# Loading q and k of a chunked-attention and mixture-of-experts kernel with eight tokens of one head pair in a partition

## The chip, the cores and the metric

The kernel runs on one core of a Trainium2 chip. The metric is the device time of one execution in microseconds (us), lower is better. A core has a matrix engine (TensorE; its matmuls are PE in the profile and its weight loads PEld), a vector engine (DVE), a scalar engine (ACT), GpSimd (POOL) and a sync engine (SP). Each takes its instructions in program order. Transfers between the chip's memory (HBM) and SBUF, the on-chip memory of 128 partitions, run on 16 DMA engines that all issuing engines share. Here SP issues the loads of q and k and of the weights and the stores of the attention output, and POOL issues nearly all loads of v and all indirect transfers.

## The reference

There are three stages, all in float32: attention inside chunks of 64 tokens, a top-1 mixture of experts, and a dense two-layer network.

```python
# 8 batches, 8 heads, 576 tokens (9 chunks of 64), head size 64
scores = matmul(q_c, k_c^T) / 8          # inside each chunk of 64 tokens
attn = softmax(scores)
x = matmul(attn, v_c)                    # -> 4608 tokens x 512
idx = argmax(x @ w_gate)                 # 8 experts
y[t] = max_prob[t] * relu(x[t] @ w1[idx[t]]) @ w2[idx[t]]      # 512 -> 1024 -> 512
out = relu(y @ w_in)**2 @ w_out          # 512 -> 2048 -> 512
```

## The kernel before

The attention stage is a loop of 36 iterations, each of 128 tokens (two chunks) of all eight heads. q and k come in units of 256 tokens (four chunks), 18 in all, so one unit feeds two iterations. The order of all instructions is written out by hand: `for it in range(-3, NTILE + 1)` from line 455 gives every engine its program order, and nothing is rescheduled.

`load_qk(u)` (lines 241 to 255) fills one tile `qk` (tag `a`, four buffers) with q in its first half and k in its second. A partition holds two neighbouring tokens of all eight heads: eight runs of 2 x 64 floats, 512 bytes each. Partitions 32c to 32c+31 belong to chunk c of the unit, so one transfer fills all 128 partitions where the unit lies in one batch. A batch has nine chunks, so six of the 18 units cross the end of a batch; there `divmod` on line 248 splits q and k each into two transfers, of 32 and 96 partitions (four units) or of 64 and 64 (two units). The other 12 units are called whole below and those six split.

`regroup(z)` (lines 265 to 269) copies on POOL the q (even z) or k (odd z) of a unit into one of four slots of `by_r`, so that two heads of one token position stand side by side. `trans` (lines 271 to 304) transposes them on PE into PSUM, in two halves `hh`, and ACT or DVE copies the result into `qT` (q) or `kb` (k, with zeros between so that two heads share one matmul). Unit 0 is not regrouped: it is transposed straight from `qk`. `scores`, `expo`, `attn_t` and `pv` follow for each iteration, and `pv` stores 128 finished tokens to `x_d` from SP (line 359). `x_t`, `gate_t`, `route`, `place` and `scatter` make the routing out of them beside the loop.

The loads run ahead of the loop. Before the loop stand `load_qk(0)`, `load_qk(1)`, `load_qk(2)` and two parts of v of batch 0 (lines 386 to 420). `load_qk(u + 3)` is issued from `trans_upto` (line 453) when unit u has been transposed, so on SP it stands behind the store of `x_d` of the same iteration. `regroup` runs up to seven tiles of q or k ahead of the iteration (lines 456 to 459). `load_v` (lines 257 to 263) issues eight transfers a batch from POOL; each goes to one half of the partitions (64 of them), in runs of 256 bytes. The weights of the first experts are loaded by SP from iteration 22 on (line 487). The experts and the dense network then take the rest of the time.

Of the kernel before, what the change touches and what calls it, by code (L numbers as in the profile page):

```python
# [8 lines left out]
F32 = mybir.dt.float32  # L9
# [11 lines left out]
def kernel(ctx, tc, q, k, v, w_gate, w1, w2, w_in, w_out, out):  # L21
    nc = tc.nc
    B, H, S, D = q.shape
    NT, DM = out.shape
    NE = w_gate.shape[1]
    CH = 64
    NCB = S // CH
    NPAIR = H // 2
# [46 lines left out]
    def tl(tag, shape, dt, name):  # L75
        if tag in fixed:
            ts, n = fixed[tag]
            fixed[tag] = ts, n + 1
            t = ts[n % len(ts)].bitcast(dt)
            k = 1  # L80
            for z in shape[1:]:
                k *= z
            t = t[0:shape[0], 0:k]
            names = "abcde"[:len(shape) - 1]
            return t.rearrange(f"p ({' '.join(names)}) -> p {' '.join(names)}", **dict(zip(names, shape[1:])))
        if tag == "m":
# [67 lines left out]
    at_job, done, known = [0], [0], [min(i for i, (l, n, _) in enumerate(jobs) if n and n > 1)]  # L154
# [74 lines left out]
    def attention():  # L229
        with ExitStack() as actx:  # L230
            ps_t = actx.enter_context(tc.tile_pool(name="ps_t", bufs=4, space=PSUM))
# [2 lines left out]

            vb = [[tl("hhhhhhba"[4 * s + p], [128, NCB, 2, D + 1], F32, f"vb{s}{p}") for p in range(NPAIR)] for s in range(2)]
            kb = [tl("b", [128, NPAIR, 4, 2, CH], F32, f"kb{s}") for s in range(2)]
            by_r = tl("c", [128, 4, 2, H, D], F32, "by_r")
            xTs = tl("c", [128, 2, KD, 512], F32, "xTs")
            st = {}

            def load_qk(u):
                qk = tl("a", [128, 2, H, 2 * D], F32, f"qk{u}")
                for j, (src, nm) in enumerate(((q, "q"), (k, "k"))):
                    t = qk[:, j]
                    g = 4 * u
                    done = 0
                    while done < 4:
                        b, c = divmod(g + done, NCB)
                        n = min(4 - done, NCB - c)
                        nc.sync.dma_start(  # L250
                            out=t[32 * done:32 * (done + n)],
                            in_=src[b, :, c * CH:(c + n) * CH, :].rearrange("h (p r) d -> p h (r d)", r=2),
                        )
                        done += n
                    st[nm, u] = t

# [8 lines left out]
            def regroup(z):  # L265
                u, j = divmod(z, 2)
                if u:
                    src = st["qk"[j], u].rearrange("p h (r d) -> p r h d", r=2)
                    nc.gpsimd.tensor_copy(out=by_r[:, z % 4], in_=src)

            def trans(nm, u, hh):
                if hh == 0:
                    if nm == "q":
                        st["qT", u] = tl("b", [128, NPAIR, 128, 2], F32, f"qT{u}")
                src = st[nm, u] if hh == 0 else st.pop((nm, u))
                ps = ps_t.tile([128, 2, 2, 128], F32, tag="t", name="tq")
                if u == 0:
                    for h in range(4):
                        nc.tensor.transpose(ps[:, h // 2, h % 2, :], src[:, 4 * hh + h, :], ident)
                    for r in range(2):  # L280
                        for j in range(2):
                            i_ = ps[64 * r:64 * r + 64, :, j, :]
                            eng = nc.scalar.copy
                            if nm == "q":
                                o = st["qT", u][64 * j:64 * j + 64, 2 * hh:2 * hh + 2, :, r]
                            else:
                                eng = nc.vector.tensor_copy
                                i_ = i_.rearrange("p a (c i) -> p a c i", c=4)
                                o = kb[u % 2].rearrange("p a c j (i r) -> p a j c i r", r=2)[64 * j:64 * j + 64, 2 * hh:2 * hh + 2, j, :, :, r]
                            eng(o, i_)  # L290
                    return
                z = 2 * u + (nm == "k")
                for a in range(2):
                    for r in range(2):
                        h = 4 * hh + 2 * a
                        nc.tensor.transpose(ps[:, a, r, :], by_r[:, z % 4, r, h:h + 2, :].rearrange("p h d -> p (h d)"), ident)
                i_ = ps.rearrange("p a r i -> p a i r")
                if nm == "q":
                    nc.scalar.copy(st["qT", u][:, 2 * hh:2 * hh + 2], i_)
                else:  # L300
                    o = kb[u % 2].rearrange("p a c j (i r) -> p j a c i r", r=2)
                    i_ = i_.rearrange("p a (c i) r -> p a c i r", c=4)
                    for j in range(2):
                        (nc.vector.tensor_copy if j and u < 3 else nc.scalar.copy)(o[64 * j:64 * j + 64, j, 2 * hh:2 * hh + 2], i_[64 * j:64 * j + 64])

            def scores(i):
                u, h2 = divmod(i, 2)
                qt, kt = st["qT", u], kb[u % 2]
                ps = ps_s.tile([128, H, CH], F32, tag="s", name="sc")
                for p in range(NPAIR):  # L310
                    for c2 in range(2):
                        c = 2 * h2 + c2
                        nc.tensor.matmul(
                            ps[64 * c2:64 * c2 + 64, 2 * p:2 * p + 2, :],
                            lhsT=qt[:, p, 32 * c:32 * c + 32, :].rearrange("p i r -> p (i r)"),
                            rhs=kt[:, p, c],
                            start=True,
                            stop=True,
                        )
                mx = tl("m", [128, H], F32, "mx")  # L320
                nc.vector.tensor_reduce(mx, ps, axis=AX.X, op=ALU.max)
                at = tl("r", [128, H, CH], F32, "at")
                nc.vector.tensor_tensor(out=at, in0=ps, in1=mx[:, :, None].to_broadcast([128, H, CH]), op=ALU.subtract)
                st["at", i] = at
# [91 lines left out]
            c = min(6, NCB)  # L416
# [14 lines left out]
            for g in range(NG - 1):  # L431
                t = 4 * g + (7 if g < NG - 3 else 6)
# [22 lines left out]
            for it in range(-3, NTILE + 1):  # L455
# [8 lines left out]
                if 0 <= it + 1 < NTILE:  # L464
                    scores(it + 1)
# [659 lines left out]
```

## Time and profile before

| what | value |
|---|---|
| median of three runs | 1461.23 us (1460.78 to 1465.03) |
| the profiled execution's own time | 1460.37 us |
| its span, first to last instruction | 1458.5 us |
| matmul (PE) busy | 1419.3 us, 97% of the span |
| attention loop, first score matmul to last `pv` | about 10.6 to 184 us |
| mean granted TensorE clock | 0.993 |

The page gives busy times for the whole span and then the span in 40 slices of 36.5 us; the first five slices are the attention stage. A digit is a busy share in tenths. Under the slices stands what the DMA engines moved in each, in GB/s. A window of the trace is a stretch of time from the span's start. Where the text speaks of a line, L250 is line 250 of the kernel before.

### The profile page before, as it was taken

The page shows a single profiled execution, that of the slowest core. Times are in us where ns is not written, and L with a number is a line of the kernel's source. Part 1 is how long each engine was busy: PE and PEld are TensorE (multiplying, and loading weights), DVE is VectorE, ACT ScalarE, POOL GpSimd, SP SyncE. Part 2 cuts the span into 40 slices and gives each one's busy share as a digit, 9 for nine tenths or more (in the row PEclk, how much of TensorE's full clock was granted, in tenths as well). Part 3 has the DMA queues.
Part 4 walks back from the last instruction along what each step waited for, and adds up shares of the span by engine and source line. Part 5 has one row for each costly group of instructions (what it writes and reads, how often), then busy time and mean ns, then how long its engine had stood idle before and what let it go on. Part 6 is the DMA issues. An engine that isn't in the chain of part 4 may idle for free.

```text
span 1458.5 us, 21568 instructions
## 1 busy us (share of the span) xinstructions
PE 1419.3 (97%) x8186; PEld 1222.9 (84%) x8186; DVE 761.5 (52%) x1371; ACT 549.6 (38%) x936; POOL 505.6 (35%) x608
## 2 busy tenths in 40 slices
PE   7988988999999999999999999999999999999998
PEld 5877788888889999997888888888888888888886
DVE  7767787578888788884432322322332232233222
ACT  4765634444444455554422222222222222222222
POOL 7675755436555446643003040210404012040301
PEclk9999999999999999999999999999999999999999
DMA  9999555767678778885101010100101001010000
GB/s 204 260 259 244 148 162 182 221 192 234 208 225 247 223 234 266 268 257 163 58 15 46 1 60 0 44 17 1 60 0 60 0 26 35 1 60 0 31 2 29
DMA packets 144369, 172.90 MB, mean 119 GB/s; under 512 B 18160, under 2 KB 103872, under 8 KB 144256
## 3 DMA queue, kind: packets, MB, share of 16 engines
q1 hardware_dynamic: 110032, 112.58, 27.0%
q0 software_dynamic: 17920, 40.51, 10.0%
q10 hardware_dynamic: 16304, 18.36, 3.8%
q8 instruction: 65, 1.06, 0.3%
q14 instruction: 48, 0.39, 0.1%
HBM read 133.05 MB, written 38.34 MB: 118 GB/s over the span
## 4 chain that ended last, share of the span: by engine, by line
PE 54%; POOL 0%; POOLq 0%; issue 0%; DVE 0%
PE hp L1034 27%; PE py L1055 27%; POOL out_dram L1015 0%; POOLq L1120 0%; DVE o L1063 0%; POOL between L1014 0%
## 5 line engine op out<-in xcount | busy, mean ns | idle before, releaser
L1034 PE MATMUL hp<-xm,w_None 128*128 128x512 f32 x1728 | 417.5, 391 | 3.3 <-DVEq L978 3.3
L1034 PEld LDWEIGHTS hp<-xm,w_None 128*128 128x128 f32 x1728 | 326.3, 189 | 71.5 <-ACTq L978 3.5
L1055 PE MATMUL py<-w_None,h 128*128 128x512 f32 x1512 | 363.2, 389 | 0.0
L1055 PEld LDWEIGHTS py<-w_None,h 128*128 128x128 f32 x1512 | 283.8, 188 | 58.8
L1039 DVE SCALAR_TENSOR_TENSOR rs<-hp,rs 128x512 f32<-128x512 f32 x144 | 99.5, 691 | 437.7 <-ACT rs L1038 437.7
L1038 ACT ACTIVATE rs<-hp 128x512 f32<-128x512 f32 x144 | 86.0, 597 | 460.0 <-PE hp L1034 460.0
L1015 POOL DMA_INDIRECT out_dram<-o,tp x36 | 35.1, 974 | 630.2 <-ACT o L1061 624.2
L796 PE MATMUL pa<-xs,w 128*128 128x256 f32 (+2 forms) x1344 | 242.3, 329 | 5.7 <-DVE h L800 2.4
L808 PE MATMUL pb<-h,w 128*128 128x256 f32 (+2 forms) x1344 | 243.9, 331 | 0.0
L796 PEld LDWEIGHTS pa<-xs,w 128*128 128x128 f32 x1344 | 211.4, 189 | 23.5 <-DVE h L800 4.8
L808 PEld LDWEIGHTS pb<-h,w 128*128 128x128 f32 x1344 | 209.9, 190 | 14.5
L1041 DVE TENSOR_TENSOR h<-rs,h 128x512 fp32r<-128x512 f32 x144 | 99.7, 692 | 99.0 <-ACT h L1040 99.0
L190 DVE TENSOR_TENSOR w<-raw,w 128x1024 fp32r<-128x1024 f32 x100 | 132.0, 1321 | 17.1 <-ACT w L189 15.3
L799 ACT ACTIVATE h<-pa 128x256 fp32r<-128x256 f32 (+2 forms) x112 | 53.2, 475 | 215.5 <-PE pa L796 185.4
L1040 ACT CAST h<-rs 128x512 fp32r<-128x512 f32 x144 | 89.5, 622 | 110.3 <-DVE rs L1039 110.3
L189 ACT CAST w<-raw 128x1024 fp32r<-128x1024 f32 x113 | 118.1, 1046 | 0.0
L844 POOL TENSOR_TENSOR cr<-cr 128x256 f32<-128x256 f32 x64 | 49.7, 777 | 124.8 <-DVE cr L859 46.6
L800 DVE SCALAR_TENSOR_TENSOR h<-pa,h 128x256 fp32r<-128x256 f32 (+2 forms) x112 | 59.5, 534 | 59.7 <-ACT h L799 55.1
L845 POOL TENSOR_TENSOR cr<-cr 128x256 f32<-128x256 f32 x64 | 73.6, 1149 | 5.0
L223 POOL DMA_INDIRECT xg<-x_d,tk x40 | 44.6, 1115 | 28.1 <-PE pt L785 17.7
L1055 PE MATMUL py<-w,h 128*128 128x512 f32 x216 | 51.7, 389 | 0.0
L210 POOL DMA_INDIRECT tk<-tk_d,at x40 | 41.7, 1042 | 22.1 <-issue 8.5
(204 smaller groups left out, 1325.0 us busy)
## 6 DMA issues: line engine op xcount, KB each, us to landing
raw<-in_moe_w_dram SPq DMA_DIRECT2D x112, 512.0 KB, 4.1
x_d<-x SPq DMA_DIRECT2D x36, 256.0 KB, 6.8
x<-y_d POOLq DMA_DIRECT2D x36, 256.0 KB, 3.0
cr<-in_moe_w_in_dram SPq DMA_DIRECT2D x32, 256.0 KB, 4.2
cr<-in_moe_w_out_dram SPq DMA_DIRECT2D x32, 256.0 KB, 5.5
vb<-in_v_dram POOLq DMA_DIRECT2D x56, 144.0 KB, 8.2
qk<-in_q_dram SPq DMA_DIRECT2D x12, 512.0 KB, 10.1
qk<-in_k_dram SPq DMA_DIRECT2D x12, 512.0 KB, 12.2
```

Source lines behind the costliest of these rows:

```text
L189: nc.scalar.copy(w[0], raw)
L190: eng.tensor_tensor(out=w[1], in0=raw, in1=w[0], op=ALU.subtract)
L796: nc.tensor.matmul(ps[:, 0:N], lhsT=w[wl][:, kk, o:o + 128], rhs=xT[:, xl, kk, 0:N], start=(kk == 0 and wl + xl == 0), stop=(kk == KD - 1 ...
L800: nc.vector.scalar_tensor_tensor(out=h[:, 1, 0:N], in0=ps[:, 0:N], scalar=0.0, in1=h[:, 0, 0:N], op0=ALU.max, op1=ALU.subtract)
L808: nc.tensor.matmul(pb[d][:, 0:N], lhsT=w[wl][:, f % 2, 128 * d:128 * d + 128], rhs=h[:, hl, 0:N], start=(f + hl + wl == 0), stop=(f == NF ...
L845: nc.gpsimd.tensor_tensor(out=af, in0=af, in1=ef, op=ALU.add)
L1034: nc.tensor.matmul(ps, lhsT=w[wl][:, kk, o:o + 128], rhs=xT[:, xl, kk, :], start=(kk == 0 and wl + xl == 0), stop=(kk == KD - 1 and wl == 1))
L1038: nc.scalar.activation(out=rs[:, 0], in_=ps, func=AF.Relu)
L1039: nc.vector.scalar_tensor_tensor(out=rs[:, 1], in0=ps, scalar=0.0, in1=rs[:, 0], op0=ALU.max, op1=ALU.mult)
L1040: nc.scalar.copy(h[:, 0], rs[:, 1])
L1041: nc.vector.tensor_tensor(out=h[:, 1], in0=rs[:, 1], in1=h[:, 0], op=ALU.subtract)
L1055: nc.tensor.matmul(ys[t], lhsT=h[:, hl, 128 * t:128 * t + 128], rhs=w[wl][:, g % 2, :], start=(g == 0 and hl + wl == 0), stop=(g == NF2 - ...
```

## The change

`load_qk` puts eight neighbouring tokens of one pair of heads in a partition. A partition then holds two runs (one a head) of 8 x 64 floats, 2048 bytes each. The pair, a, selects the group of 32 partitions (32a to 32a+31), and inside it eight partitions belong to each chunk. A transfer can no longer fill all partitions at once, so each of the former transfers becomes four, one a pair: 32 partitions each in a whole unit; 8 and 24, or 16 and 16, in a split one. `by_r`, the transposes and the copies behind them follow the new order: the half `hh` now selects four of the eight token positions for all heads, where it selected four heads. The number and size of the copies on POOL, ACT and DVE and of the transposes stay as they were; `qT` is now plain in token order, and `scores` reads it so.

```diff
-            by_r = tl("c", [128, 4, 2, H, D], F32, "by_r")
+            by_r = tl("c", [128, 4, 8, 2, D], F32, "by_r")
...
-                qk = tl("a", [128, 2, H, 2 * D], F32, f"qk{u}")
+                qk = tl("a", [128, 2, 2, 8 * D], F32, f"qk{u}")
...
-                        nc.sync.dma_start(
-                            out=t[32 * done:32 * (done + n)],
-                            in_=src[b, :, c * CH:(c + n) * CH, :].rearrange("h (p r) d -> p h (r d)", r=2),
-                        )
+                        for a in range(NPAIR):
+                            nc.sync.dma_start(
+                                out=t[32 * a + 8 * done:32 * a + 8 * (done + n)],
+                                in_=src[b, 2 * a:2 * a + 2, c * CH:(c + n) * CH, :].rearrange("h (p r) d -> p h (r d)", r=8),
+                            )
...
-                    src = st["qk"[j], u].rearrange("p h (r d) -> p r h d", r=2)
+                    src = st["qk"[j], u].rearrange("p h (r d) -> p r h d", r=8)
...
-                        st["qT", u] = tl("b", [128, NPAIR, 128, 2], F32, f"qT{u}")
+                        st["qT", u] = tl("b", [128, NPAIR, 256], F32, f"qT{u}")
...
-                for a in range(2):
-                    for r in range(2):
-                        h = 4 * hh + 2 * a
-                        nc.tensor.transpose(ps[:, a, r, :], by_r[:, z % 4, r, h:h + 2, :].rearrange("p h d -> p (h d)"), ident)
-                i_ = ps.rearrange("p a r i -> p a i r")
+                for r in range(4):
+                    nc.tensor.transpose(ps[:, r], by_r[:, z % 4, 4 * hh + r].rearrange("p h d -> p (h d)"), ident)
+                i_ = ps.rearrange("p r n -> p n r")
+                w = slice(4 * hh, 4 * hh + 4)
                 if nm == "q":
-                    nc.scalar.copy(st["qT", u][:, 2 * hh:2 * hh + 2], i_)
+                    nc.scalar.copy(st["qT", u].rearrange("p a (g r) -> p (a g) r", r=8)[:, :, w], i_)
...
-                            lhsT=qt[:, p, 32 * c:32 * c + 32, :].rearrange("p i r -> p (i r)"),
+                            lhsT=qt[:, p, 64 * c:64 * c + 64],
```

## Rows read from the trace of the kernel before

**Rows 1.** The page: engine busy times and the span in 40 slices.

```profile
PE 1419.3 (97%) x8186; PEld 1222.9 (84%) x8186; DVE 761.5 (52%) x1371; ACT 549.6 (38%) x936; POOL 505.6 (35%) x608
...
DMA  9999555767678778885101010100101001010000
GB/s 204 260 259 244 148 162 182 221 192 234 208 225 247 223 234 266 268 257 163 58 15 46 1 60 0 44 17 1 60 0 60 0 26 35 1 60 0 31 2 29
```

**Rows 2.** Windows, attention stage: busy us and instructions by engine, clock, DMA share, GB/s.

```profile
12.00:36.00 24.00, 20.23 (x220) 17.20 (x221) 15.89 (x37) 10.11 (x20) 17.53 (x31) 1.00 1.21 208
36.00:73.00 37.00, 36.95 (x449) 31.76 (x449) 26.37 (x64) 28.42 (x52) 22.53 (x31) 1.00 1.09 259
73.00:109.00 36.00, 32.16 (x385) 27.73 (x380) 24.78 (x61) 21.67 (x39) 27.29 (x38) 0.95 1.10 260
109.00:146.00 37.00, 33.32 (x379) 29.47 (x376) 29.21 (x67) 20.88 (x39) 22.08 (x31) 0.91 0.94 244
```

**Rows 3.** Groups by line, 0 to 165 us: busy, mean ns, idle before and releaser.

```profile
L296 PE MATMUL tq<-ident,by_r 128*128 128x128 f32 x272 | 42.4, 285 | 4.5 <-POOL by_r L269 4.5
L304 ACT COPY kb<-tq 64x512 f32<-64x512 f32 x62 | 35.9, 579 | 4.6 <-PE tq L296 3.9
L269 POOL COPY by_r<-qk 128x1024 f32<-128x1024 f32 x34 | 35.0, 1050 | 31.3 <-DMA qk<-in_q_dram 18.9 <-DMA qk<-in_k_dram 5.5 <-PE pv L346 3.6
L299 ACT COPY qT<-tq 128x512 f32<-128x512 f32 x34 | 20.1, 590 | 6.7 <-PE tq L296 6.6
L336 ACT COPY aT<-ta 128x512 f32<-128x512 f32 x32 | 18.8, 586 | 48.3 <-PE ta L334 31.0 <-DVE mx L321 8.4 <-DVE ei L517 4.9
L279 PE MATMUL tq<-ident,qk 128*128 128x128 f32 x16 | 3.9, 425 | 5.2 <-DMA qk<-in_q_dram 5.2
```

**Rows 4.** The page, DMA issues: KB each, median us from issue to landing.

```profile
vb<-in_v_dram POOLq DMA_DIRECT2D x56, 144.0 KB, 8.2
qk<-in_q_dram SPq DMA_DIRECT2D x12, 512.0 KB, 10.1
qk<-in_k_dram SPq DMA_DIRECT2D x12, 512.0 KB, 12.2
```

**Rows 5.** Timeline of SP's queue: start us, us, issues; units 2, 4, 16 and 17.

```profile
10.80 2.92 SPq L250 DMA_DIRECT2D qk<-in_q_dram  x2
13.76 1.84 SPq L250 DMA_DIRECT2D qk<-in_k_dram  x2
...
21.35 2.62 SPq L250 DMA_DIRECT2D qk<-in_q_dram  x2
24.02 3.43 SPq L250 DMA_DIRECT2D qk<-in_k_dram  x2
...
130.01 0.38 SPq L250 DMA_DIRECT2D qk<-in_q_dram  x1
130.44 1.15 SPq L250 DMA_DIRECT2D qk<-in_k_dram  x1
...
142.70 0.41 SPq L250 DMA_DIRECT2D qk<-in_q_dram  x1
143.16 1.46 SPq L250 DMA_DIRECT2D qk<-in_k_dram  x1
```

**Rows 6.** Windows in which one kind of transfer runs nearly alone; columns as rows 2.

```profile
15.80:19.20 3.40, 2.75 (x28) 2.34 (x24) 1.78 (x3) 1.90 (x5) 2.60 (x8) 1.00 1.22 213
30.50:33.20 2.70, 2.08 (x20) 1.68 (x18) 1.96 (x5) 1.36 (x3) 1.53 (x3) 1.00 1.22 206
141.40:142.80 1.40, 1.40 (x16) 1.40 (x14) 1.33 (x4) 1.30 (x3) 0.00 (x0) 1.00 1.14 295
154.30:156.80 2.50, 2.50 (x35) 2.46 (x35) 2.33 (x6) 1.98 (x4) 2.50 (x4) 1.00 1.02 195
117.00:120.80 3.80, 1.77 (x25) 1.58 (x27) 3.52 (x10) 3.12 (x6) 0.00 (x0) 0.78 0.01 4
```

**Rows 7.** DMA totals, 30.5:33.2, 148.3:150 and 126.5:128.5 us: packets, MB, mean GB/s.

```profile
DMA packets 1119, 0.56 MB, mean 206 GB/s; under 512 B 41, under 2 KB 1118, under 8 KB 1119
...
DMA packets 621, 0.59 MB, mean 347 GB/s; under 512 B 60, under 2 KB 424, under 8 KB 621
...
DMA packets 625, 0.69 MB, mean 345 GB/s; under 512 B 37, under 2 KB 521, under 8 KB 625
```

**Rows 8.** Timeline of POOL and PE at the last unit: start us, us, instructions.

```profile
151.16 5.96 POOL L260 DMA_DIRECT2D vb<-in_v_dram  x8
157.06 2.08 POOL L269 COPY by_r<-qk 128x1024 f32<-128x1024 f32 x2
...
164.14 0.60 PE L296 MATMUL tq<-ident,by_r 128*128 128x128 f32 x4
```

**Rows 9.** Issues and landings of the lines L250, L359: duration ns min/median/max, times.

```profile
L250 SPq DMA_DIRECT2D qk<-in_q_dram x24: 378/521/1826, 0.8 to 142.7; - x24
L250 SPq DMA_DIRECT2D qk<-in_k_dram x24: 313/1148/6107, 1.3 to 143.2; - x24
...
L359 SPq DMA_DIRECT2D x_d<-x x36: 319/384/7757, 27.6 to 191.6; - x36
...
DMA to landing us min/median/max: 2.0/6.8/13.9
```

More of the change, by code (lines that the diff above doesn't have):

```diff
@@ L273, in trans @@
                     if nm == "q":
-                        st["qT", u] = tl("b", [128, NPAIR, 128, 2], F32, f"qT{u}")
+                        st["qT", u] = tl("b", [128, NPAIR, 256], F32, f"qT{u}")
                 src = st[nm, u] if hh == 0 else st.pop((nm, u))
-                ps = ps_t.tile([128, 2, 2, 128], F32, tag="t", name="tq")
+                ps = ps_t.tile([128, 4, 128], F32, tag="t", name="tq")
                 if u == 0:
-                    for h in range(4):
-                        nc.tensor.transpose(ps[:, h // 2, h % 2, :], src[:, 4 * hh + h, :], ident)
+                    for h in range(2):
+                        for a in range(2):
+                            nc.tensor.transpose(ps[:, 2 * h + a], src[:, h, 256 * hh + 128 * a:256 * hh + 128 * a + 128], ident)
@@ L280, in trans @@
                     for r in range(2):
                         for j in range(2):
-                            i_ = ps[64 * r:64 * r + 64, :, j, :]
-                            eng = nc.scalar.copy
+                            i_ = ps[64 * r:64 * r + 64, 2 * j:2 * j + 2].rearrange("p a n -> p n a")
+                            w = slice(4 * hh + r, 4 * hh + r + 3, 2)
                             if nm == "q":
-                                o = st["qT", u][64 * j:64 * j + 64, 2 * hh:2 * hh + 2, :, r]
-                            else:
-                                eng = nc.vector.tensor_copy
-                                i_ = i_.rearrange("p a (c i) -> p a c i", c=4)
-                                o = kb[u % 2].rearrange("p a c j (i r) -> p a j c i r", r=2)[64 * j:64 * j + 64, 2 * hh:2 * hh + 2, j, :, :, r]
@@ L290, in trans @@
-                            eng(o, i_)
+                                o = st["qT", u].rearrange("p a (g r) -> p (a g) r", r=8)[64 * j:64 * j + 64, :, w]
+                                nc.scalar.copy(o, i_)
+                            else:
+                                o = kb[u % 2].rearrange("p a c j (i r) -> p (a c) j i r", r=8)[64 * j:64 * j + 64, :, j, :, w]
+                                nc.vector.tensor_copy(o, i_.rearrange("p (c i) a -> p c i a", i=8))
                     return
@@ L298, in trans @@
+                w = slice(4 * hh, 4 * hh + 4)
                 if nm == "q":
-                    nc.scalar.copy(st["qT", u][:, 2 * hh:2 * hh + 2], i_)
+                    nc.scalar.copy(st["qT", u].rearrange("p a (g r) -> p (a g) r", r=8)[:, :, w], i_)
                 else:
-                    o = kb[u % 2].rearrange("p a c j (i r) -> p j a c i r", r=2)
-                    i_ = i_.rearrange("p a (c i) r -> p a c i r", c=4)
+                    o = kb[u % 2].rearrange("p a c j (i r) -> p j (a c) i r", r=8)
+                    i_ = i_.rearrange("p (c i) r -> p c i r", i=8)
@@ L303, in trans @@
                     for j in range(2):
-                        (nc.vector.tensor_copy if j and u < 3 else nc.scalar.copy)(o[64 * j:64 * j + 64, j, 2 * hh:2 * hh + 2], i_[64 * j:64 * j + 64])
+                        (nc.vector.tensor_copy if j and u < 3 else nc.scalar.copy)(
+                            o[64 * j:64 * j + 64, j, :, :, w], i_[64 * j:64 * j + 64])
             def scores(i):
```

## The prediction

> **What bounds the kernel now.** I read the page first [rows 1]. PE is busy for 97% of the span, and the change touches only the attention stage, the first five slices. There PE's digits drop to 7 and 8 while the DMA engines stand at 9 for four slices at 204 to 260 GB/s. So this is the one stage in which a change to loads could show. The windows say the same [rows 2]: from 12 to 146 us the DMA share is about 1 all the time, and PE is idle for 3.8 of 24 us, 0.05 of 37, 3.8 of 36 and 3.7 of 37. In the window without idle time PE runs 449 instructions in 37 us; that is the pace PE would keep, and with some 50 of them in an iteration it is about 4.2 us an iteration or 8.4 us a unit. The granted clock is 0.95 and 0.91 in the two windows after it, because short stops drop PE to the lower of its two levels for a while.
>
> Then the question was how much of PE's idle time is due to q and k. The groups by line answer it [rows 3]: `regroup` on POOL (L269) waits 18.9 us for q and 5.5 us for k, but PE waits only 4.5 us for `regroup` (L296), and 5.2 us for the very first load (L279). So the loads of q and k are just ahead of PE. Faster loads can win little; slower ones are felt once a small lead is used up.
>
> **What the loads run at.** SP's queue is worked off in order, so a stretch with little but 512-byte packets can be given to a unit by the issues before it [rows 5]. Unit 2 is split 32 and 96, unit 4 is split 64 and 64, and units 16 and 17 are whole. The rates in their stretches are 213 GB/s (15.8 to 19.2 us, unit 2, with a little of v), 206 (30.5 to 33.2 us, unit 4) and 295 (141.4 to 142.8 us, unit 16) [rows 6]. All are 512-byte runs, the first two in transfers to a part of the partitions, the last in transfers to all 128. Nearly all of the 1119 packets of the second stretch lie in the 512-byte class [rows 7]. v goes to 64 partitions in 256-byte runs and moves alone at 195 GB/s (154.3 to 156.8 us) [rows 6]. So on 64 partitions a run twice as long gains 5%, while 128 instead of 64 partitions gain 43%. With 128 partitions and longer runs (stores of 2048-byte rows, and weights) the rate is 347 and 345 GB/s [rows 7]. I conclude that the rate of a transfer to part of the partitions is set by how many partitions it reaches, hardly by the length of its runs. The change lengthens the runs and cuts the partitions from 128 to 32.
>
> The Trainium skill has this as a rule that speaks against the change: its page "SBUF — State Buffer", section "Door 1: The DMA port swizzle (why [64,N] ≈ [32,N])", says that the rate of a transfer depends on how many of 16 ports its partitions reach, that partitions 0 to 63 reach no more of them than 0 to 31, and that two transfers to different halves do not add up. The trace agrees as far as it goes, with 206 against 295 GB/s. The page's 189 GB/s for 32 partitions would make the whole units below 66.7 us instead of 61.2.
>
> **The change part by part.** Each unit is 1.05 MB of q and k (512.0 KB each of q and k) [rows 4].
>
> (1) Whole units, 12, together 12.6 MB. Before: 12.6 / 0.295 = 42.7 us of DMA time. After, in pieces of 32 partitions: the nearest row is the 206 GB/s of 64 partitions, and the 32-partition quarter inside unit 2 shows no worse than that with 213. 12.6 / 0.206 = 61.2 us, so +18.5 us. The bound below: if run length counted after all, 12.6 / 0.347 = 36.3 us, so -6.4 us.
>
> (2) Split units, six, together 6.3 MB. Before: 6.3 / 0.209 (the mean of 213 and 206) = 30.1 us. After, in pieces of 16, or 8 and 24, partitions, which no row shows. The bounds are the rate of 64 partitions kept (30.6 us, +0.5) and half of it, in proportion to the partitions (6.3 / 0.103 = 61.2 us, +31.1). I take one more step of the size seen from 128 to 64 partitions: 206 / 295 = 0.70, and 0.70 x 206 = 144 GB/s, 43.8 us, +13.7 us. It lies between the ends, and the step down is the only trend that rows show.
>
> (3) Slack that swallows some of it. The DMA engines stand idle for 3.8 us at 117 to 120.8 us [rows 6], waiting for SP. The last unit is issued by 144.6 us [rows 5], and with some 10 us to landing [rows 4] it is there at about 153 us. POOL takes it only at 157.06 us, after the issues of v, and PE has it all by 164.1 us [rows 8], so a lead of about 6 us is left there. Together 9.8 us.
>
> (4) More issues on SP: 48 become 12 x 8 + 6 x 16 = 192. An issue takes 0.31 to 0.38 us when nothing is full [rows 9], so 2.8 us for a whole unit and 5.6 us for a split one, within the 8.4 us of a unit. Behind them on SP stand the stores of `x_d`, which today land after 6.8 us in the middle and 13.9 us at most [rows 9], with four `x` buffers, 16.8 us at 4.2 us each. I price this at nothing as long as that cover holds; if stores land 5 us later than the worst of today, `pv`'s last step waits some 2 us in each such iteration.
>
> (5) The first load: q of unit 0 is four issues and 0.52 MB at 206 GB/s, about 2.5 us instead of 1.8, and PE's first wait of 5.2 us [rows 3] grows by about 1 us, k's landing by 1.6. This is part of (1) and not counted again.
>
> (6) Copies and transposes. Their counts and sizes stay. The copies read PSUM with a stride already: 590 ns for `qT` (L299) against 586 ns for the plain copy `aT` of the same size (L336) [rows 3], so a stride costs nothing there. `regroup` moves the same 16 runs of 64 floats (1050 ns). I put all this at nothing. If writing four of every eight floats cost 50 ns on each of the 34 + 62 copies of ACT, that is 4.8 us on an engine that is busy for 21 to 28 us of 37 [rows 2], so it stays beside PE.
>
> The sum is +18.5 + 13.7 - 9.8 = +22.4 us. PE waits for it inside the loop, so everything behind the loop moves by the same amount; experts and network have no slack that gives it back, since PE stands at 9 there [rows 1]. Against the profiled execution's 1460.4 us that is 1482.8 us; the median of the runs is 0.9 us above that execution, so 1483 us and a little, say 1484.
>
> **The rivals.** First, small pieces cost in full: pieces of 16 or fewer partitions run at 103 GB/s, the upper bound of (2). Then +18.5 + 31.1 - 9.8 = +39.8 us, 1501 us. For it speaks that nothing in the rows shows a floor below 64 partitions; against it that the 32-partition parts inside unit 2 did not lower its rate to anything like half. The Trainium skill's table in the same section has 104 GB/s for 16 partitions at 1 MiB, and by it this rival would be the one.
>
> Second, faster: the rate goes by run length, and 2048-byte runs move at 347 GB/s. Then all 18.9 MB take 54.5 us instead of 72.8. Of the 18 us PE can only get back what it waits, 4.5 us and under 1 us of the first load, and some of the clock lost after those stops: about -5 us, 1456 us. It decides once a piece of 32 partitions runs above 295 GB/s. Against it stand v's 195 and unit 4's 206 GB/s.
>
> Third, hidden: the pieces of neighbouring pairs, which go to different halves of the partitions, overlap on the engines so that the whole rate stays near 260 GB/s. Then the added 14 us or less go mostly into the 9.8 us of slack: 0 to +4 us, 1462 us. Against it: unit 4's transfers already alternate between the halves and stay at 206.
>
> Fourth, the stores are caught behind the loads as in (4) and DVE, too, waits: +50 us or more.
>
> **How the numbers follow.** Less than 0.3% (4.4 us) can't be told from no change. Forecast (1468 to 1492): 0.50. Small pieces in full (1492 to 1510): 0.22. Hidden, within 0.3%: 0.10. Faster, under 1457: 0.10. Stores caught, above 1510: 0.08. Faster 0.10, same 0.10, slower 0.80. For the range I leave out the stores at the top and most of the faster case at the bottom: 1458 to 1507.
>
> **What would show it.** In the profile after: packets of 2048 bytes for q and k; stretches of them at about 200 GB/s, lower in split units; a DMA share near 1 up to 160 us and beyond; `regroup` waiting for q and k for well over the 24.4 us of today; PE waiting for `regroup` 20 us or more instead of 4.5; the last `regroup` at about 180 us instead of 157. Steps (4) and (6) are wrong if DVE waits for stores, or if L299 or L304 get longer. The prediction fails as a whole if stretches of q and k run at 290 GB/s or more, or if PE's wait for `regroup` stays under 8 us.

## The result, and the profile after

The changed kernel takes 1482.65 us (median, 1477.6 to 1488.53); the kernel before, run beside it, 1462.45 us. The ratio is 1.0139, 95% interval 1.0114 to 1.0164: slower by 20 us. The forecast was 1484 us. The experiments below show that the number was met by errors that cancel; that it came so close is luck.

The page of after, engine busy times and the 40 slices (of 37.0 us here; as [rows 1]):

```profile
PE 1421.2 (96%) x8186; PEld 1225.3 (83%) x8186; DVE 763.1 (52%) x1371; ACT 550.4 (37%) x936; POOL 510.2 (34%) x608
...
PE   6799779999999999999999999999999999999998
...
DMA  9899836757767778885301010010101001010000
GB/s 173 198 241 227 209 111 209 195 172 228 237 218 224 244 224 258 264 262 184 113 1 59 1 52 8 15 45 1 59 0 50 10 6 54 1 59 0 30 2 29
```

The PE digits of before:

```profile
PE   7988988999999999999999999999999999999998
```

PE has the same 8186 matmuls. What differs lies in the first slices: PE's digits fall from 7 and 9 to 6 and 7 in the first two and from 9 and 8 to 7 in the fifth and sixth. In the first two slices the DMA engines moved 173 and 198 GB/s instead of 204 and 260, and in the fifth they still stand at 8, where they had been through with the loads and at 5 [rows 1]. Windows of the attention stage of after (columns as [rows 2]), four for the stretches shown of before, then one up to the start of the last `regroup`:

```profile
12.00:36.00 24.00, 18.23 (x180) 15.87 (x181) 14.44 (x34) 8.07 (x16) 16.39 (x29) 0.93 1.00 168
36.00:73.00 37.00, 27.27 (x311) 23.75 (x310) 19.06 (x44) 19.10 (x35) 13.07 (x15) 0.95 0.88 191
73.00:109.00 36.00, 35.45 (x420) 30.76 (x419) 26.56 (x61) 24.30 (x44) 29.11 (x41) 0.96 0.96 245
109.00:146.00 37.00, 33.38 (x392) 28.91 (x392) 26.26 (x65) 23.50 (x43) 24.66 (x36) 0.95 0.90 222
...
0.00:178.49 178.49, 143.66 (x1602) 123.82 (x1602) 117.06 (x275) 96.19 (x175) 110.83 (x172) 0.95 0.92 213
```

The loss is greatest from 36 to 73 us: PE was busy for 27.27 us, where before it was for 36.95 [rows 2]. In that window the DMA share is 0.88 on the mean, where it had been 1.09. So for a part of the time the engines that move the data had too little to move.

The timeline of POOL in after has the last `regroup` (as [rows 8]):

```profile
178.49 2.07 POOL L270 COPY by_r<-qk 128x1024 f32<-128x1024 f32 x2
```

It starts 21.4 us later than the 157.06 us of before [rows 8], and the span is 21.9 us longer. So all of the loss arises before that point, and nothing of it comes back. The same stretch of before for comparison:

```profile
0.00:157.06 157.06, 138.69 (x1584) 119.54 (x1586) 113.53 (x267) 94.01 (x172) 110.52 (x171) 0.97 1.05 241
```

PE's idle time up to there went from 157.06 - 138.69 = 18.4 us to 178.49 - 143.66 = 34.8 us, 16.4 us more. PE's busy time is 5.0 us longer. Some 1.6 us of it are 18 more matmuls recorded by then; the other 3.4 us are longer ones (143.66 / 1602 = 89.7 ns a piece, 87.6 before), at a mean granted clock of 0.95 in place of 0.97.

Groups by line in after, 0 to 190 us (columns as [rows 3]; most line numbers are one higher than before's, and L295 is before's L296):

```profile
L295 PE MATMUL tq<-ident,by_r 128*128 128x128 f32 x272 | 43.3, 288 | 16.7 <-POOL by_r L270 16.6
L304 ACT COPY kb<-tq 64x512 f32<-64x512 f32 x64 | 37.1, 580 | 9.5 <-PE tq L295 8.8
L270 POOL COPY by_r<-qk 128x1024 f32<-128x1024 f32 x34 | 35.3, 1052 | 61.2 <-DMA qk<-in_k_dram 25.9 <-DMA qk<-in_q_dram 14.8 <-PE pv L347 14.1
L299 ACT COPY qT<-tq 128x512 f32<-128x512 f32 x34 | 20.1, 590 | 15.3 <-PE tq L295 15.2
L281 PE MATMUL tq<-ident,qk 128*128 128x128 f32 x16 | 3.9, 426 | 6.7 <-DMA qk<-in_q_dram 5.3 <-DMA qk<-in_k_dram 1.4
```

PE waits 16.6 us for `regroup` (4.5 before), and `regroup` 40.7 us for q and k (24.4 before). The copies last what they did: 580, 1052 and 590 ns against 579, 1050 and 590 [rows 3].

The timeline of SP's queue in after (columns as [rows 5]) shows two split units, each of eight issues for q and eight for k, and then a whole one:

```profile
32.16 4.82 SPq L251 DMA_DIRECT2D qk<-in_q_dram  x8
38.28 7.19 SPq L251 DMA_DIRECT2D qk<-in_k_dram  x8
45.56 0.84 SPq L360 DMA_DIRECT2D x_d<-x  x2
...
51.60 4.49 SPq L251 DMA_DIRECT2D qk<-in_q_dram  x8
56.13 5.01 SPq L251 DMA_DIRECT2D qk<-in_k_dram  x8
...
73.12 1.84 SPq L251 DMA_DIRECT2D qk<-in_q_dram  x4
75.00 1.84 SPq L251 DMA_DIRECT2D qk<-in_k_dram  x4
```

This whole unit is eight issues in 3.7 us. A split unit is 16. These two take 13.3 us (32.16 to 45.47) and 9.5 us (51.60 to 61.14), the other four 9.7, 8.8, 8.4 and 6.8 us. The mean of the six is 9.4 us, more than the 8.4 us in which the prediction let PE use up a unit. Unit 4, the first one shown, is also late from its start: its q is issued from 32.16 us on, in before from 21.35 us [rows 5]. It is what PE waits for in its longest stop for `regroup`, 5.2 us up to 45.6 us.

Taken one by one, the first four issues of k of this unit are short, and the time lies between them:

```profile
38.28 0.31 SPq L251 DMA_DIRECT2D qk<-in_k_dram  x1
39.60 0.31 SPq L251 DMA_DIRECT2D qk<-in_k_dram  x1
41.10 0.31 SPq L251 DMA_DIRECT2D qk<-in_k_dram  x1
43.29 0.31 SPq L251 DMA_DIRECT2D qk<-in_k_dram  x1
```

The trace's semaphores tell what SP does there. As all these kernels are built, the transfers that SP and ACT issue share eight semaphores, used in turn, and an issue stands until the transfer that used its semaphore last, eight issues earlier, has landed. The four above start 17 ns after the first four pieces of q have landed, which took 6.1 to 9.2 us from their issue. So no more than eight transfers are under way at a time. By themselves the 16 issues of a split unit last 4.7 to 6.5 us, 5.6 on the mean; the waits between them for an earlier landing add 1.0 to 7.5 us, 3.4 on the mean.

This is how the DMA engines stood while SP was in the middle of such a unit, and then, in after, in a run below ("The same issues and partitions, with short runs") and in before, a stretch near the start in which q and k move alone (columns as [rows 2]):

```profile
43.00:47.50 4.50, 1.86 (x9) 1.87 (x10) 0.00 (x0) 0.71 (x2) 1.04 (x1) 0.77 0.58 175
...
4.00:5.00 1.00, 0.00 (x0) 0.00 (x0) 0.73 (x4) 0.00 (x0) 1.00 (x2) 1.00 1.00 219
4.00:5.00 1.00, 0.00 (x0) 0.00 (x0) 0.73 (x4) 0.00 (x0) 1.00 (x2) 1.00 1.15 183
4.00:4.80 0.80, 0.00 (x0) 0.00 (x0) 0.68 (x3) 0.00 (x0) 0.80 (x2) 1.00 1.16 326
```

In the first, the DMA engines are 58% busy, and PE is idle for 2.6 of 4.5 us waiting for q of this unit. The granted clock, part of the time at the lower of its two levels after the stop, is 0.77. In the other three the engines are full. 2048-byte runs to 32 partitions move at 219 GB/s, 512-byte runs to 32 partitions at 183, and 512-byte runs to 128 partitions at 326. The prediction had taken 206 for the first and 295 for the last.

Last, issues of the two loads in after, and the issues and the waiters of the store (as [rows 9]):

```profile
L251 SPq DMA_DIRECT2D qk<-in_q_dram x96: 272/376/1407, 0.8 to 166.4; - x96
L251 SPq DMA_DIRECT2D qk<-in_k_dram x96: 272/312/1496, 2.6 to 168.3; - x96
...
L360 SPq DMA_DIRECT2D x_d<-x x36: 319/359/1325, 45.6 to 212.9; - x36
...
  DVE x L359: 9.3, 3
  POOL by_r L270: 4.4, 2
```

Half of the issues last 0.31 or 0.38 us and less, as the prediction took from before [rows 9]. The ones in the rows of eight above come to 0.56 to 0.90 us each with the gaps between them. The longest issue of a store lasted 7.8 us before [rows 9], and that one began only when its rows were ready; now it is 1.3, and DVE waits 9.3 us for stores that stand behind loads.

The waits of SP's queue, 0 to 175 us (engine and line, whom it waited for, us in total, times, longest), first the longest row of before, then the longest two of after:

```profile
SPq L359 <- DVE x L358: 38.9, 13, 7.0
...
SPq L251 <- DMA qk<-in_q_dram: 17.2, 28, 1.9
SPq L251 <- DMA qk<-in_k_dram: 16.8, 24, 1.4
```

Before, SP was ahead and waited for DVE to finish the rows that it stores. After, it has no such row among its longest; its loads wait for earlier loads. All its waits for transfers come to 61 us there, and to none in before.

### The profile page after: what moved, and what is told of

It is laid out like the page before. It is cut to its first block, busy times and chain, and to the rows that moved or that the text cites. A ratio compares the mean times of both kernels' runs of the same rounds, so it can differ in the third digit from the quotient of the medians.

```text
span 1480.4 us, 21790 instructions
## 1 busy us (share of the span) xinstructions
PE 1421.2 (96%) x8186; PEld 1225.3 (83%) x8186; DVE 763.1 (52%) x1371; ACT 550.4 (37%) x936; POOL 510.2 (34%) x608
## 4 chain that ended last, share of the span: by engine, by line
PE 53%; POOL 0%; POOLq 0%; issue 0%; DVE 0%
PE hp L1035 27%; PE py L1056 26%; POOL out_dram L1016 0%; POOLq L1121 0%; DVE o L1064 0%; POOL between L1015 0%
## 5 line engine op out<-in xcount | busy, mean ns | idle before, releaser
L295 PE MATMUL tq<-ident,by_r 128*128 128x128 f32 x272 | 43.3, 288 | 16.7 <-POOL by_r L270 16.6
L270 POOL COPY by_r<-qk 128x1024 f32<-128x1024 f32 x34 | 35.3, 1052 | 61.2 <-DMA qk<-in_k_dram 25.9
```

## The experiments

The expectations name three theories by letters. A is the prediction's: the rate is set by how many partitions a transfer reaches, so whole units lose too. B: the number of issues is what costs. C: the pieces of the split units are slow because they are small or reach few partitions, and whole units lose next to nothing. All times are set against before on the same chip: 1469.59 us for the two runs with changes to the split units only, for the one with twice as many issues and for the one with a second engine; 1460.97 for the one with tiny issues, the two with one issue and the one half way; 1460.63 for the first four. Where I give a number of us for a run, it is the difference of these medians.

### Loads alone

Before's compute, with after's loads (the tile is viewed in after's shape, so the tokens stand in another order).

```diff
+                    tw = t.rearrange("p (h x) e -> p h (x e)", h=2)
...
-                            out=t[32 * done:32 * (done + n)],
-                            in_=src[b, :, c * CH:(c + n) * CH, :].rearrange("h (p r) d -> p h (r d)", r=2),
+                            out=tw[32 * a + 8 * done:32 * a + 8 * (done + n)],
+                            in_=src[b, 2 * a:2 * a + 2, c * CH:(c + n) * CH, :].rearrange("h (p r) d -> p h (r d)", r=8),
```

> The loads of the changed kernel (32, or 8 and 24, or 16 and 16 partitions, 2048-byte runs) with everything else as in the kernel before, so q and k stand in another order in the tile and the attention weights are wrong. Theory A (the partitions a transfer reaches set its rate), theory B (the number of issues on SP sets it) and theory C (only the pieces below 32 partitions cost anything) all expect the changed kernel's time, 1483 us, within 4. Only if the new order of transposes and copies had a cost of its own would it be below 1479.

1482.25 us, ratio 1.0154 (1.0119 to 1.0188). The loads carry the whole loss. The new transposes and copies cost nothing that can be seen.

### Whole units only

After, with each split unit loaded as four whole chunks of one batch: no piece of fewer than 32 partitions, 144 issues in place of 192.

```diff
-                        n = min(4 - done, NCB - c)
+                        c, n = min(c, NCB - 4), 4
```

> The changed kernel with the six split units loaded as if they were whole: four chunks from inside one batch, so for these units some tokens are wrong, but bytes and the 32-partition pieces of 2048-byte runs are as in a whole unit, and no piece is smaller. Theory A by the terms of the prediction: +18.5 for whole units, +0.5 for the others, less 9.8 of slack, +9 us, 1471 us. Theory B: 144 issues instead of 192, two thirds of the increase stays, 1476 us. Theory C: the whole increase goes, 1460 to 1464 us.

1464.5 us, ratio 1.0022 (1.0008 to 1.0036). Twelve former whole units, and six more, in eight transfers of 32 partitions each, cost about 4 us. A and B as first stated, with a loss in every unit, both fall; what is lost is lost in the split units. PE's wait for `regroup` is 6.9 us. SP waits for earlier landings here too, 58 us in all, but with these waits a unit's eight issues take longer than 8.4 us in two of 18 units only. In the window from 36 to 73 us the DMA engines are full again:

```profile
36.00:73.00 37.00, 34.28 (x393) 29.44 (x389) 25.34 (x58) 24.15 (x44) 21.47 (x27) 0.95 1.04 254
```

### The same issues and partitions, with short runs

Before, with each chunk a transfer of its own: 32 partitions and eight issues in every unit, as in the run above, but 512 bytes a run.

```diff
-                        n = min(4 - done, NCB - c)
+                        n = 1
```

> The kernel before with each load of q and k cut into four transfers of one chunk, 32 partitions each, 512-byte runs, 144 issues, none smaller than 32 partitions. Theory A: 32 partitions at 206 GB/s, 1471 us, like new_unsplit since the run length does not matter. Theory B: 1476 us. Theory C: 1460 to 1464 us. If runs of 512 bytes in small pieces are slower than runs of 2048 bytes, it comes out above new_unsplit.

1472.92 us, ratio 1.0079 (1.0049 to 1.0109). Against the run above only the length of the loads' runs differs, and it is worth some 8 us. The time by itself fits A's 1471 and B's 1476 alike; it is the pair of runs that tells. So A's "hardly by the length of its runs" is wrong on 32 partitions. The window of 36 to 73 us:

```profile
36.00:73.00 37.00, 33.72 (x402) 30.16 (x399) 24.28 (x57) 22.97 (x43) 20.12 (x25) 0.95 1.14 243
```

The DMA engines are busier (1.14 against 1.04) and move less (243 against 254 GB/s). This is the case that the prediction had reckoned with: engines that are full and slow.

### More issues, with partitions and runs as before

Before, each transfer cut by pairs of heads: 192 issues as in after, to the partitions of before, 512 bytes a run.

```diff
-                                out=t[32 * done:32 * (done + n)],
+                                out=t[32 * done:32 * (done + n), 2 * a:2 * a + 2],
```

> The kernel before with each of its transfers cut into four, one for each pair of heads: partitions as before (128 in whole units, 32 and 96 or 64 and 64 in split ones), 512-byte runs, 192 issues as in the changed kernel. Theory A: no change, 1460 to 1464 us. Theory B: the whole increase, 1483 us. Theory C: 1460 to 1464 us.

1477.33 us, ratio 1.0121 (1.009 to 1.0152). With no change of partitions, this is within the interval of after's 1.0139. The number of issues has to count; with the run of whole units, it has to count mainly in the split ones.

### Only the split units: small pieces, or many issues?

Two runs with whole units as in before, and split units in 16 issues. In the first they are after's pieces (8 to 24 partitions); in the second, whose edit is shown, they are cut by pairs (32, 64 or 96 partitions, 512 bytes a run).

```diff
+                        for hs in ([slice(0, H)] if n == 4 else [slice(2 * a, 2 * a + 2) for a in range(NPAIR)]):
-                                out=t[32 * done:32 * (done + n)],
-                                in_=src[b, :, c * CH:(c + n) * CH, :].rearrange("h (p r) d -> p h (r d)", r=2),
+                                out=t[32 * done:32 * (done + n), hs],
+                                in_=src[b, hs, c * CH:(c + n) * CH, :].rearrange("h (p r) d -> p h (r d)", r=2),
```

> The kernel before, whole units untouched (one transfer of 128 partitions each for q and k), and only the six split units loaded as in the changed kernel: 16 issues a unit, pieces of 8 and 24 or 16 and 16 partitions, 2048-byte runs (tokens of these units in another order, so their attention weights are wrong). By the terms of the prediction (theory A): +13.7 less 9.8, about +4 us, 1465 us. Theory B (a unit of 16 issues is held up by SP, 0.46 us an issue) and theory C (pieces below 32 partitions are slow by themselves) both expect the increase of the changed kernel less the 4 us that new_unsplit kept: 1476 to 1481 us.

> As split_small, whole units untouched, but the six split units cut by pairs of heads: the same 16 issues a unit and the same 64 KB on average in each, to 32 and 96 or 64 and 64 partitions as in the kernel before, 512-byte runs. Theory B: the same as split_small, 1474 to 1481 us. Theory C: no piece is below 32 partitions, so no increase, 1460 to 1464 us. Theory A: the same as theory C.

1479.33 us, ratio 1.008 (1.0048 to 1.0112), and 1479.96 us, ratio 1.0071 (1.0045 to 1.0097). They are the same within their intervals. So a loss of this size needs no piece below 32 partitions, and C, which expected none in the second run, falls. That the partitions do nothing isn't shown by it: from the first run to the second the runs also shrank from 2048 to 512 bytes, and the two could offset each other. What both share is 16 issues a unit. The expectations were written against some 1461 us; as increases, B's were +15 to +20 and +13 to +20 us, and both runs (+9.7 and +10.4) stay below them. SP's queue in the second, at a split unit:

```profile
26.31 8.93 SPq L251 DMA_DIRECT2D qk<-in_q_dram  x8
35.81 5.89 SPq L251 DMA_DIRECT2D qk<-in_k_dram  x8
```

### Issues without bytes

Before, with three tiny transfers behind each piece of a split unit: its real pieces are untouched, and each of these units has 16 issues.

```diff
+                        if n < 4:
+                            for a in range(3):
+                                nc.sync.dma_start(out=scr[...], in_=src[b, a, 0:16, 0:2])
```

> Before, with three tiny transfers on SP (16 runs of 8 bytes, into a tile that nobody reads) behind each transfer of a split unit: 12 more issues in each of the six split units, 120 in all, and no change in what q and k move or in where it goes. Theory B (a split unit is slow because SP needs 9 to 10 us for 16 issues, longer than PE's 8.4 us for a unit): SP's time for the loads grows by 72 x 0.4 to 0.5 us = 29 to 36 us, all of it in split units, and the time by +5 to +12 us, near split_by_pair's 0.7%; a little less than there, since the last tiny transfers stand behind the last real one. Rival C (the real pieces are slow to move, the issues only wait for them): 0 to +3 us, and PE's wait for regroup stays at 4 to 7 us.

1472.32 us, ratio 1.0076 (1.0056 to 1.0095): +11.4 us, as much as when the real pieces were cut. It is in the upper part of what B allowed, and far from C's 0 to 3. PE's wait for `regroup` is 15.4 us. How long the tiny issues lasted (columns as [rows 9]), and one split unit on SP's queue:

```profile
L261 SPq DMA_DIRECT2D scr<-in_q_dram x36: 310/418/1836, 12.2 to 131.3; - x36
L261 SPq DMA_DIRECT2D scr<-in_k_dram x36: 310/418/1007, 18.6 to 136.1; - x36
...
38.02 0.60 SPq L252 DMA_DIRECT2D qk<-in_k_dram  x1
38.67 1.91 SPq L261 DMA_DIRECT2D scr<-in_k_dram  x3
40.62 0.60 SPq L252 DMA_DIRECT2D qk<-in_k_dram  x1
41.27 1.54 SPq L261 DMA_DIRECT2D scr<-in_k_dram  x3
```

A transfer of 128 bytes takes SP as long (418 ns in the middle) as a piece of 32 to 128 KB in after (376 and 312 ns), or longer. The issue has a price of its own. It also holds one of the eight places like any other: the tiny transfers landed 4.7 us after their issue, in the middle. So this run shows that the count of issues costs, with bytes, runs and partitions as before, but not how much of it is the issue and how much the place.

### Twice as many issues for every unit

The run of whole units, with each piece cut in two by head: 16 issues of 64 KB in all 18 units, none of fewer than 32 partitions.

```diff
+                            for h in range(2):
-                                out=t[32 * a + 8 * done:32 * a + 8 * (done + n)],
+                                    out=t[32 * a + 8 * done:32 * a + 8 * (done + n), h],
```

> new_unsplit with each of its pieces cut in two by head: 32 partitions, one run of 2048 bytes in each, 64 KB a piece, 16 issues in every unit, 288 in all, no piece below 32 partitions. Theory B: every unit is now held up as the six split ones are, 1.05 MB in 7.4 us of issues alone, and with three times as many such units the increase is at least that of the changed kernel, 1485 us or more. Theory C: as new_unsplit, 1462 to 1467 us.

1505.86 us, ratio 1.0249 (1.0215 to 1.0283). Here every unit is what only the split ones are in after. A window in the middle of it (columns as [rows 2]):

```profile
92.00:110.00 18.00, 16.97 (x199) 14.19 (x198) 12.87 (x32) 10.61 (x20) 7.23 (x10) 0.94 0.54 162
```

The DMA engines are half idle; in the whole stage POOL waits 65.0 us for q and k, and PE 20.5 us for POOL. Eight issues a unit cost 4 us for the whole kernel; 16 cost 36. SP's waits for earlier landings are only 17 us of the first 170 here, while its 292 issues in that time last 133 us by themselves: with 16 issues in every unit their own time nearly fills SP.

### A second engine to issue

After, with k of the split units issued by ACT.

```diff
-                            nc.sync.dma_start(
+                            (nc.scalar if n < 4 and nm == "k" else nc.sync).dma_start(
```

> The changed kernel with k's pieces of the six split units issued by ACT instead of SP; pieces, partitions and runs are the same. Theory B: SP has 8 issues a split unit like in a whole one, the other 8 go on beside them: most of the increase goes, 1464 to 1471 us. Theory C: the pieces are as small as before, 1479 to 1485 us. Against both: ACT's own issues, some 0.4 us each, 48 in all, may delay its copies.

1500.54 us, ratio 1.0223 (1.0187 to 1.026): worse than after, and outside what either theory expected. Timelines of ACT's and SP's queues at one split unit:

```profile
55.68 0.31 ACTq L251 DMA_DIRECT2D qk<-in_k_dram  x1
...
57.16 4.03 ACTq L251 DMA_DIRECT2D qk<-in_k_dram  x5
61.23 0.59 ACT L299 COPY qT<-tq 128x512 f32<-128x512 f32 x1 [3.69 <-DMA qk<-in_k_dram]
...
56.23 7.53 SPq L251 DMA_DIRECT2D qk<-in_q_dram  x8
```

With the gaps, an issue took 0.8 to 0.9 us in these rows (4.03 / 5 and 7.53 / 8), but single issues lasted 0.27 to 0.42 us on both engines. The rest is waiting. SP and ACT share the eight semaphores, so that each now waits for landings of the other's transfers: SP's second issue stood until 57.69 us for the piece that ACT had issued at 55.68, its third until 60.29 us for ACT's next. The 16 were through no sooner than from SP alone. And ACT's copies, which the loop needs, stood behind its issues: `qT` sat for 3.69 us. What the two engines share here is thus the eight places; whether two engines would help with places of their own was not tried. The Trainium skill, page "DMA: Bandwidth & Descriptors", section "Issuing engines are not separate DMA queues", says that issuing from several engines only saves the time to initiate the transfers, "which is usually small relative to the DMA itself". In after it isn't small: the 16 issues of a split unit last 5.6 us on the mean, and one of its pieces lands 2.4 to 9.9 us after its issue. And here nothing of it was saved.

### One issue, with and without long runs

Before with no split units, and the same with 2048-byte runs on all 128 partitions (36 issues in both).

```diff
-                        n = min(4 - done, NCB - c)
+                        c, n = min(c, NCB - 4), 4
...
-                            out=t[32 * done:32 * (done + n)],
-                            in_=src[b, :, c * CH:(c + n) * CH, :].rearrange("h (p r) d -> p h (r d)", r=2),
+                            out=t.rearrange("p (h x) e -> p h (x e)", h=2),
+                            in_=src.rearrange("b h s d -> (b h s d)")[131072 * u:131072 * u + 131072].rearrange("(h p e) -> p h e", h=2, p=128),
```

> Before, with the split units loaded as four chunks of one batch in one transfer (so with wrong tokens): 36 issues instead of 48, all of 128 partitions, 512-byte runs. The floor that a load without splits would have. Theory B (issues) and theory A (partitions) both expect little, since before's split units have four issues, 2.5 to 6 us, within the pace, and PE waits only 4.5 us for regroup: -5 to 0 us. If it is faster by 8 us or more, the split units cost before something that neither theory has.

> Before's compute, but each of q and k of a unit is one transfer of 128 partitions with two runs of 2048 bytes (consecutive tokens of two heads, so wrong tokens): the change's run length with neither its more issues nor its fewer partitions; 36 issues. To be compared with old_unsplit, which differs by run length alone. If run length counts on 128 partitions, its packets move at 300 GB/s or more and the DMA share in 36 to 109 us is under 1.0; the time is at most 5 us better, since PE waits for little: -6 to 0 us against before, within 3 us of old_unsplit. A slower time would mean that long runs by themselves hurt other transfers (v, weights).

The first hunk alone: 1460.78 us, ratio 0.9985 (0.9973 to 0.9998). Both hunks: 1456.59 us, ratio 0.9975 (0.9961 to 0.9989). Both times lie in the ranges expected. By their ratios the two are 0.1% apart, by their medians 4.2 us, a little over the 3 us expected. The longer runs do what the change is built on: the share of the DMA engines for about the same bytes falls from the 1.09, 1.10 and 0.94 of before [rows 2] to

```profile
36.00:73.00 37.00, 36.95 (x454) 32.07 (x454) 26.68 (x64) 28.35 (x52) 26.06 (x34) 1.00 0.95 270
73.00:109.00 36.00, 33.29 (x388) 28.52 (x385) 28.44 (x64) 22.12 (x40) 25.38 (x37) 0.95 0.78 215
109.00:146.00 37.00, 34.34 (x422) 29.57 (x421) 30.23 (x69) 24.07 (x45) 22.92 (x34) 1.00 0.86 262
```

But PE is the bound and had waited only 4.5 us for `regroup`; this wait is 1.1 us in the first run and gone in the second. That is about the most that faster loads of q and k can give in the loop, 0.3%.

### Half way

Before's compute with four tokens of four heads in a partition: 1024 bytes a run, two issues for each one of before, so eight in a split unit.

```diff
+                        for a in range(2):
-                                out=t[32 * done:32 * (done + n)],
+                                out=tw[64 * a + 16 * done:64 * a + 16 * (done + n)],
```

> Before's compute with loads half way to the change: four tokens of four heads in a partition, 1024 bytes a run, each former transfer cut in two (64 partitions in whole units; 16 and 48, or 32 and 32, in split ones; tokens in another order), 96 issues. Theory B (issues against the pace): a split unit has 8 issues, 4 to 5 us of SP, under the 8.4 us of a unit; so hardly any loss: -2 to +5 us, PE's wait for regroup 4 to 8 us. Theory A (partitions and piece sizes): half way or more to after's 1.4%: +8 to +16 us.

1465.72 us, ratio 1.0035 (1.0022 to 1.0049): +4.8 us, at the upper edge of B's range and well below A's. PE's wait for `regroup`, 8.7 us, is just above the 4 to 8 expected. With eight issues or fewer in a unit it stays near the run of whole units.

## Why the prediction was right, and where it was not

**The time and its sign** were right, and the place: nothing but the loads (loads alone, +21.6 us), all of it in the attention loop, handed on through `regroup` to PE, with no slack behind it. `regroup` waits 40.7 us for q and k where "well over 24.4" was said; the last one starts at 178.49 us where about 180 was. PE's wait for it is 16.6 us, a little under the 20 named.

**Step (1), whole units, was over-sized.** +18.5 us of DMA time less 9.8 us of slack is +8.7 us; the run of whole units has +3.9 us. Alone, q and k do move slowly on 32 partitions, at 219 GB/s against 326 on 128; that the partitions count was right. But in the loop they share the engines with v and the stores: from 36 to 73 us the run of whole units moved 254 GB/s, before 259 [rows 2]. What also failed is the conclusion that the rate depends hardly on run length, with 183 GB/s for 512 and 219 for 2048 bytes. It came from 256- and 512-byte runs on 64 partitions [rows 6] and was carried over to 2048 bytes. With 512 bytes on 32 partitions the loss is real (+12.3 us, engines full at 1.14); with 2048 bytes most of it is gone. The rows of longer runs, 347 and 345 GB/s [rows 7], were of 128 partitions, and were put down to partitions alone. The Trainium skill's 189 GB/s for 32 partitions (page "SBUF — State Buffer", section "Door 1: The DMA port swizzle (why [64,N] ≈ [32,N])"), named beside this step, is below the 219 GB/s of 4 to 5 us; pieces to several groups of partitions moved there together, so that isn't one transfer's rate, and no run here has one such transfer alone.

**Step (4), issues at nothing, is the step that failed.** The count of 192 was right, and so was the price of the issues themselves: 16 x 0.35 = 5.6 us for a split unit "within 8.4", and they last 5.6 us on the mean. The prediction put nothing for SP's waits between them. It had taken the issue "when nothing is full", and here the eight places are full: SP stands 1.0 to 7.5 us of a split unit until an earlier transfer has landed. The unit's 16 issues then take 6.8 to 13.3 us, 9.4 on the mean, which puts SP over PE's pace. SP falls behind, q of unit 4 is issued 10.8 us later than before, and between 43 and 47.5 us the DMA engines run dry at 0.58. The sign "a DMA share near 1" did not come: it is 0.92 up to the last `regroup`, 1.05 before. Three kinds of split units with 16 issues, small pieces, pairs and tiny transfers, give +9.7, +10.4 and +11.4 us. That the count of issues costs is shown by these runs. How the cost divides between the issues' own time and the waits is read from the traces, and no run changes one of them alone.

**Step (2), split units, had a fair size for the wrong reason.** +13.7 us stands against 9.7 to 11.4 measured, which is luck. The small number of partitions, by which it was worked out, isn't needed for such a loss (pairs and tiny transfers have the partitions of before); whether it adds to it is not shown. The bound of "half, in proportion to the partitions", the rival of 0.22, has the same flaw.

**What is not settled.** Whole units alone (+3.9) and split units alone (+9.7) add up to 14 us, and after lost 20. The same holds for cutting by pairs: +10.4 in the split units, +16.7 in all. The likely reason is the order on SP: before, SP waited for DVE at the stores, 38.9 us in 13 waits, and in such time it can catch up after a split unit; in after hardly any is left, as the whole units' eight issues have taken it. This is argued from the rows and was not tried by itself. Waits for a landing cost only where they make a unit's issues outlast PE's pace: the run of whole units has 58 us of them and after 61. Nor was it tried what more than eight places would give, or why some issues last longer than 0.3 to 0.4 us without such a wait: 6.1 us at most among before's loads [rows 9].

**Steps (3), (5) and (6).** The slack was used up, as said. The first wait grew from 5.2 to 6.7 us, as said. Copies and transposes cost nothing (590, 580 and 1052 ns). The stores, a rival of 0.08, did come late in a small way: DVE waits 9.3 us for them, 0.4 before, and PE's `pv` 5.7 us for DVE, 4.1 before. The prediction had named that wait as the mark by which step (4) would be seen to be wrong, and so it was. The faster rival fell with its condition, rates above 295 GB/s on 32 partitions (219 where they move alone with the engines full); the run with one long-run issue shows that even where the DMA time does fall, PE has only 4 us to win.

## What to carry to other kernels

When a layout lengthens the runs by cutting a transfer into pieces, count the issues of the worst unit, not of the mean one, price each as a row of issues lasts in a trace with its gaps (0.4 to 0.8 us in a split unit here, not the shortest single one), and set that against the time in which the unit is used up. Look up how many transfers may be under way at once, eight here: cutting each into four leaves a quarter of the bytes under way. Where the DMA share is under 1 while the consumer waits, look when the awaited transfer was issued; longer runs don't bring a late issue forward. And look first at how long the bound engine waits for the load at all: here 4.5 us, so the change could win 0.3% at most, and lost 1.4%.

## What the hardware showed that was not expected

- Up to 128 KB an issue's length doesn't follow the size of the transfer: 418 ns in the middle for 128 bytes, 312 and 376 ns for pieces of 32 to 128 KB. Before's issues, of up to 512 KB, lasted 521 and 1148 ns in the middle [rows 9].
- A small transfer holds its place nearly as long as a large one: 128 bytes landed after 4.7 us in the middle, after's pieces of q and k after 4.5 us.
- Two engines that issue at once wait for each other's transfers where they share the semaphores: 0.8 to 0.9 us an issue with the gaps, 0.27 to 0.42 us without.
- At 32 partitions run length matters: 512 against 2048 bytes, with the same 144 issues, 1.0079 and 1.0022, and 183 against 219 GB/s alone.
